# Inverse transforms fed by GpSimd: the second product over x's spectrum, raw weights behind GpSimd's additions, one output by SyncE, stores of v ahead of loads

## The chip, the cores and the metric

The kernel runs on one core of one Trainium2 chip. The metric is the device time of one execution in microseconds (us); lower is better. Matrix products run on TensorE (PE in the profile, PEld its weight loads), elementwise work on VectorE (DVE), ScalarE (ACT) and GpSimd (POOL), and SyncE (SP) issues most of the transfers. Each engine takes its own instructions strictly in the order in which the program has them.

## The reference

Two branches work on the same normalised input and are summed: a long convolution (S4D) done by FFT, and a gated feed-forward layer (GLU). There are 2048 positions, D = 448 channels, N = 256 states and F = 1792 hidden units, all in float32.

```python
xn = _layernorm(x, axis=-1)                     # x: [1, 2048, 448]
# S4D
P = jnp.exp((A * dt[:, None])[:, :, None] * pos[None, None, :])
K = 2.0 * jnp.einsum("dn,dnl->dl", C, P).real   # kernel of 2048 taps per channel
Kf, Uf = jnp.fft.rfft(K, 2 * L), jnp.fft.rfft(u_t, 2 * L)
y = jnp.fft.irfft(Uf * Kf[None, :, :], 2 * L)[:, :, :L]
# GLU
h = sigmoid(xn @ w_gate) * (xn @ w_up)
return x + (y + xn * D_skip) + h @ w_down
```

## The kernel before, in words

The program has two generators, `conv` and `glu`, whose instructions are interleaved by a planner: each `yield` names a cost, and the generator that is further behind its total goes on. A scheduler then orders the instructions of each engine by priority and by the pairs that `tc.issue_after` fixes.

The GLU runs over two halves of the positions (each two blocks `t` of 512) and over F in chunks `f` of 128 hidden units. For each pair (f, t) `gate` makes two sums of 11 matmuls of 128x512 (gate and up, tile `gu`, L710). Float32 is split into a high part and a remainder, so each weight chunk has two tiles, `wh` and `wl`, and of the 11 matmuls the first four read `wh`, the next four `wl`. The down projection reads `dh` and `dl` in the same way (tile `po`, L831). In the first half the split weights of some chunks are stored and read back later. The chunks in `RAW` (0, 1, 2, 4, 5) are not: in the second half their raw weights are loaded again by GpSimd's queue (`wraw`, `rdw`), and GpSimd makes `wh` by a copy and `wl` by a subtraction (L774, L775), and `dh`, `dl` alike (L802, L803). They are the last five chunks of the second half, in the order 4, 5, 0, 1, 2, and the code below makes each of them just ahead of the gate that reads it first.

The convolution first makes the taps (until about 530 us), and then `spectra` does the transforms beside the GLU's last chunks. It has 17 steps (h, k), numbered 0 to 16 here: h is the half of the channels, k a group of four frequency blocks; step 1 is the odd one (None, 32), with 64 rows. A step has these parts:

- `there` (L902): 64 small matmuls turn the loaded rows `skl` and `sx` into the spectra of taps and x in the two PSUM tiles `pk` and `px`; ScalarE copies the odd parts (`oo`), and VectorE makes `kk` and `xx` (L924, L925).
- `product` (L929): two VectorE products over 896 columns (L931, L932), then a subtraction and an addition of 448 columns on GpSimd (L934, L935) give the complex product `yy`. The second product is written over `kk`, of which there is one buffer.
- `halves` (L938): VectorE makes `sd` from `yy` (L940, L941), one step later.
- `back` (L944): 32 matmuls on `sd` go back to the time side, again into `pk` and `px`; ScalarE copies them to `vt`, and SyncE stores `vt` to `v_d` in DRAM (L973).
- `turned` (L975): SyncE reads rows of two steps back as `vp`, and `last` (L981) does the final matmuls (L989) and adds the result to `acc`, which `out` and `out_end` store.

On TensorE the order of a step is `there` of step n, one or two gate sums or down products, `back` of step n-2, more of the GLU, and so on; this order is fixed by the `issue_after` marks `sp_mm` and `glu_mm`.

Of the kernel before, what the change touches and what calls it, by code (L numbers as in the profile page):

```python
# [15 lines left out]
ALU = mybir.AluOpType  # L16
# [24 lines left out]
H = D // 2  # L41
# [86 lines left out]
def s4d_glu_kernel(ctx, tc, io):  # L128
    nc = tc.nc
    hp = tc.high_priority  # L130
    v = nc.vector
# [565 lines left out]
    def gate(w, xs, to, between=None):  # L697
# [30 lines left out]
            v.tensor_tensor(hl, hf, hh, ALU.subtract)  # L728
        to.append((hh, hl))

    def glu():
        stores, later, coming, coming_d = [], [], {}, {}
        last_fs = [f for fs_ in ORDER[1] for f in fs_]
        follow = dict(zip(last_fs, last_fs[1:]))
        for half in range(2):
# [4 lines left out]
            for fs_ in ORDER[half]:  # L740
# [14 lines left out]
                for n_, (f, t) in enumerate(order):  # L755
                    if t == 0:
                        wh = pg.tile([128, 2, 4, 128], F32R, name="wh", bufs=2)
                        if half == 0:
                            first = len(raws) == 2
                            raw, rd = raws.pop()  # L760
                            wl = w_low()
                            with hp(HP):
                                nc.scalar.copy(wh, raw)
                                if first:
                                    v.scalar_tensor_tensor(wl, raw, lim[:, 0, 0:1], wh, ALU.mult, ALU.subtract)
                                else:
                                    v.tensor_tensor(wl, raw, wh, ALU.subtract)
                            if not raws and f + 1 < NFT:
                                raws.append((w_load(f + 1), None))
                            if f not in RAW:  # L770
                                stores.extend(kept((wh, wl), wt_d, f))
                        elif f in RAW:
                            raw, wl = coming.pop(f), w_low()
                            nc.gpsimd.tensor_copy(wh, raw)  # L774
                            nc.gpsimd.tensor_tensor(wl, raw, wh, ALU.subtract)  # L775
                        else:
                            wl = w_low()
                            for t_, d_ in kept((wh, wl), wt_d, f):
                                nc.sync.dma_start(t_, d_)
                        if half == 1 and follow.get(f) in RAW:  # L780
                            coming[follow[f]] = w_load(follow[f], eng=nc.gpsimd)
                        ws.append((wh, wl))
                    between = (lambda s_=mid[n_]: step(*s_)) if cross and mid[n_] else None
                    yield from gate(ws[f - f0], xq[2 * half + t], hs[t], between)
                    for t_, d_ in stores:
                        nc.sync.dma_start(d_, t_)
                    stores[:] = later
                    later.clear()
                    if t == 0:
                        dh = pg.tile([128, D], F32R, name="dh", bufs=FCH[0])  # L790
                        if half == 0:
                            rd = rd or rd_load(f)
                            dl = d_low()
                            with hp(HP), tc.issue_after((act if f == 1 else marks)[0].ins):
                                nc.scalar.copy(dh, rd)
                            nc.gpsimd.tensor_tensor(dl, rd, dh, ALU.subtract)  # L796
                            if f not in RAW:
                                later.extend(kept((dh, dl), dt_d, f))
                        elif f in RAW:
                            dl = d_low()  # L800
                            rd = coming_d.pop(f)
                            nc.gpsimd.tensor_copy(dh, rd)  # L802
                            nc.gpsimd.tensor_tensor(dl, rd, dh, ALU.subtract)  # L803
                        else:
                            dl = d_low()
                            for t_, d_ in kept((dh, dl), dt_d, f):
                                nc.sync.dma_start(t_, d_)
                        if half == 1 and follow.get(f) in RAW:
                            rd = pg.tile([128, D], F32, name="rdw", bufs=1)
                            coming_d[follow[f]] = rd_load(follow[f], rd, nc.gpsimd)  # L810
                        wts.append((dh, dl))
                    yield 2.5
                    for s_ in end[n_] if cross else ():
                        step(*s_)
                    if cross:
                        yield 2
# [38 lines left out]
    def spectra(pf):  # L855
# [16 lines left out]
        def work(n, sh, bufs):  # L872
            return spare[n].pop() if spare.get(n) else pf.tile(sh, F32, name=n, bufs=bufs)
# [28 lines left out]
        def there(k, tb, sk, sx):  # L902

            n = 2 if k == 32 else 4
            np_ = 32 * n
            both = []
            for j, src in enumerate((sk, sx)):
                with after():
                    for c in range(2):
                        for g in range(n):  # L910
                            for p in range(2):
                                s = slice(64 * p, 64 * p + 64)
                                to = pb[j][32 * g : 32 * g + 32, p, H * c : H * c + H]
# [4 lines left out]
                                mm = nc.tensor.matmul(to, w, rhs, start=True, stop=True, skip_group_check=True)  # L918
                sp_mm[:] = [mm]
                ev, od = (half(pb[j][:np_, p, : 2 * H]) for p in range(2))  # L920
                oo = work("oo", [128, 2, H], 2)
                nc.scalar.copy(oo[:np_], od)
                t = work(("kk", "xx")[j], [128, 2, 2, H], 1)
                v.tensor_tensor(t[:np_, 0], ev, oo[:np_], ALU.add)  # L924
                read = v.tensor_tensor(t[:np_, 1], ev, oo[:np_], ALU.subtract)  # L925
                both.append(t[:np_])
            return *both, read

        def product(np_, kk, xx, eng=nc.gpsimd):  # L929
            yy = work("yy", [128, 2, 2, H], 1)[:np_]  # L930
            v.tensor_tensor(yy, kk, xx, ALU.mult)  # L931
            v.tensor_tensor(kk, kk, xx[:, :, ::-1], ALU.mult)  # L932
            with hp(HP):
                eng.tensor_tensor(yy[:, :, 0], yy[:, :, 0], yy[:, :, 1], ALU.subtract)  # L934
                eng.tensor_tensor(yy[:, :, 1], kk[:, :, 0], kk[:, :, 1], ALU.add)  # L935
            return yy

        def halves(np_, yy):  # L938
            sd = work("sd", [128, 2, 2, H], 2)
            v.tensor_tensor(sd[:np_, 0], yy[:, 0], yy[:, 1], ALU.add)  # L940
            v.tensor_tensor(sd[:np_, 1], yy[:, 0], yy[:, 1], ALU.subtract)  # L941
            return sd

        def back(h, k, sd, engs=(nc.sync, nc.sync)):  # L944
# [30 lines left out]
        def turned(h, k, n=8):  # L975
            if h not in vp:
                vp[h] = pf.tile([128, 32, H], F32, name="vp", bufs=1)
            s = slice(k // 4, 128, n)
            nc.sync.dma_start(vp[h][s], v_d[h, s])

        def last(h, q):  # L981
# [16 lines left out]
                v.tensor_tensor(a, a, half(pb[q % 2][:, p, : 2 * H]), ALU.add)  # L998
            if h == 1 and q < 3:
                out_end(acc, 4 * q, ds, *([[nc.gpsimd]] if q == 0 else []))  # L1000
            elif h == 0 and q < 2:
                out(acc, 4 * q, h)

        ac = acl[0]
        lasts.append(last)
# [9 lines left out]
        for n, (h, k) in enumerate(steps):  # L1015
# [8 lines left out]
            prev = h, k, 64 if k == 32 else 128  # L1024
            prev += (product(prev[2], kk, xx, v if end else nc.gpsimd),)
            if (h, k) == (0, ks[-NTB - 1]):
                for k_ in ks[:-NTB]:
                    tabs.pop(k_)
# [23 lines left out]
            if due and n >= due[0]:  # L1052
                sp_mm[:] = glu_mm
                for q in (0, 1, 2, 3)[2 * (n - due[0]) : 2 * (n - due[0]) + 2]:
                    sp_mm[:] = glu_mm
                    last(0, q)
                    yield WS / 2
                if n == due[0] + 1:
                    due = []
        sp_mm[:] = glu_mm  # L1060
        back(*made)
        sp_mm[:] = glu_mm
        back(*made_, (nc.sync, nc.scalar))
        for t in (*wait, made[:2], made_[:2]):
            turned(*t)

    def conv():
        with tc.tile_pool(name="psk", bufs=1, space=PSUM) as ps_, tc.tile_pool(
# [89 lines left out]
    lasts, glu_mm, sp_mm, glu_on, outs, x1s, hfs, xls = [], [], [], [], [0], [0], [], []  # L1158
# [45 lines left out]
```

## Time and profile before

| what | value |
|---|---|
| median of 3 runs | 746.65 us (744.72 to 747.68) |
| the profiled execution | 741.93 us, of it 740.1 us from the first to the last instruction |
| granted TensorE clock, mean | 0.949 |
| busy: PE, DVE, ACT, POOL | 90%, 79%, 57%, 57% of the span |
| DMA | 114.47 MB, mean 155 GB/s |
| `spectra` on TensorE | about 541 to 703 us, then the last down products and `last` |

All times inside the run are us from the start of the span. A row of the timeline has start, length, engine, line, operation, output and input tiles with their shape, and in brackets how long the engine stood idle ahead of it and what ended that. A row of the waits reads: engine and line that waited, arrow, whom it waited for, then total us, times, and the longest. A row of the stretches (windows) gives the busy time of each engine, the granted TensorE clock (PEclk), the busy share of the DMA engines and GB/s. "Issue" as a releaser means that the profile shows none.

### The profile page before, as it was taken

To read this page: it belongs to the slowest core of one execution; us is meant where nothing else is said; L and a number is where in the kernel's file an instruction comes from. 1 tells how busy PE (TensorE), PEld (TensorE's weight loads), DVE (VectorE), ACT (ScalarE), POOL (GpSimd) and SP (SyncE) were. 2 spreads that over 40 slices of the span, in tenths; PEclk is the share of its full clock that TensorE was granted. 3 is DMA by queue.
4 is the path that set the end of the run, shared out by engine and by line. 5 is a ranking of instruction groups with operands and counts; after the bars stand their busy time and mean duration, and the time that the engine had idled before them with its cause. 6 is when DMAs were issued, how large, how long until landed. Compare 5 with 4: busy or idle time off the path is not lost.

```text
span 740.1 us, 20863 instructions
## 1 busy us (share of the span) xinstructions
PE 668.2 (90%) x8581; PEld 515.1 (70%) x8581; DVE 587.9 (79%) x779; ACT 420.6 (57%) x651; POOL 420.8 (57%) x453
## 2 busy tenths in 40 slices
PE   2998999988999999788999999999988999788976
PEld 1765878866877787555878888888765667466655
DVE  5799998699999999886679898886757777756833
ACT  3655454689778789887387777777323322222310
POOL 2120116869999999974645776765537773541301
PEclk9999999995999999999999999999998989898987
DMA  9935338451313564354863323322669887874464
GB/s 199 235 114 198 116 102 263 147 188 58 126 48 97 175 191 116 114 181 148 264 188 99 93 95 95 99 81 83 157 171 266 222 244 185 262 210 130 125 169 132
DMA packets 94335, 114.47 MB, mean 155 GB/s; under 512 B 13728, under 2 KB 83936, under 8 KB 93984
## 3 DMA queue, kind: packets, MB, share of 16 engines
q1 hardware_dynamic: 72512, 92.54, 43.1%
q10 hardware_dynamic: 19248, 14.91, 7.0%
q0 software_dynamic: 2480, 5.67, 3.0%
q8 instruction: 68, 1.11, 0.6%
q14 instruction: 27, 0.22, 0.1%
HBM read 68.32 MB, written 44.76 MB: 153 GB/s over the span
## 4 chain that ended last, share of the span: by engine, by line
PE 40%; POOL 19%; issue 11%; DVE 11%; DMA 11%; SPq 5%; ACT 3%; POOLq 0%; DVEq 0%; ACTq 0%
PE gu L710 17%; PE po L831 10%; POOL me L513 7%; PE ko L619 5%; POOL mf L513 5%; PE tr L535 2%; DMA v_d<-vt 2%; POOL dl L796 2%; DVE Ft L605 2%; DVE Et L604 1%; DMA skl<-sk_d 1%; SPq L896 1%; DMA xe<-in_A_u_dram 1%; DVE Et L603 1%; POOL yy L934 1%
## 5 line engine op out<-in xcount | busy, mean ns | idle before, releaser
L513 POOL TENSOR_TENSOR me<-me,pm 128x32 f32<-128x32 f32 (+1 forms) x168 | 149.5, 890 | 67.6 <-DVE Et L604 57.8
L513 POOL TENSOR_TENSOR mf<-mf,pm 128x64 f32<-128x64 f32 (+1 forms) x112 | 118.8, 1061 | 5.3
L710 PE MATMUL gu<-xh,wh 128*128 128x512 f32 x336 | 103.2, 415 | 3.0 <-ACT th L718 1.2
L710 PE MATMUL gu<-xl,wh 128*128 128x512 f32 x336 | 97.7, 394 | 0.0
L710 PE MATMUL gu<-xh,wl 128*128 128x512 f32 x336 | 96.5, 395 | 0.0
L604 DVE TENSOR_TENSOR Et<-me,S 128x1024 f32<-128x1024 f32 x56 | 80.4, 1436 | 13.9 <-ACT me L526 9.0
L831 PE MATMUL po<-dh,hh 128*128 128x448 f32 (+1 forms) x227 | 87.4, 385 | 0.8 <-DVE acc L836 0.8
L605 DVE TENSOR_TENSOR Ft<-mf,S 128x1024 f32<-128x1024 f32 x56 | 83.8, 1496 | 5.1 <-PE ko L619 3.2
L831 PE MATMUL po<-dh,hl 128*128 128x448 f32 (+1 forms) x227 | 84.5, 374 | 2.0 <-DVE hl L728 2.0
L831 PE MATMUL po<-dl,hh 128*128 128x448 f32 (+1 forms) x227 | 84.8, 374 | 0.2 <-POOL dl L796 0.2
L603 DVE TENSOR_TENSOR Et<-me,S 128x1024 f32<-128x1024 f32 x56 | 77.5, 1385 | 4.0 <-ACT S L546 3.5
L710 PEld LDWEIGHTS gu<-xh,wh 128*128 128x128 f32 x336 | 62.6, 195 | 25.8 <-issue 6.9
L543 ACT ACTIVATE S<-tr 128x1024 f32<-128x1024 f32 x56 | 57.9, 1033 | 34.4 <-PE tr L535 18.7
L619 PEld LDWEIGHTS ko<-Et,Ft 128*32 128x32 f32 x3584 | 56.0, 114 | 28.0 <-issue 10.5
L619 PE MATMUL ko<-Et,Ft 128*32 128x64 f32 x3584 | 66.0, 227 | 9.7 <-DVE Ft L605 5.3
L710 PEld LDWEIGHTS gu<-xh,wl 128*128 128x128 f32 x336 | 63.8, 191 | 14.9 <-DVE hl L728 0.7
L710 PEld LDWEIGHTS gu<-xl,wh 128*128 128x128 f32 x336 | 63.0, 189 | 14.8 <-issue 1.4
L726 ACT CAST hh<-gu 128x512 fp32r<-128x512 f32 x56 | 33.1, 591 | 69.8 <-DVE gu L721 68.8
L836 DVE SCALAR_TENSOR_TENSOR acc<-po,acc 128x448 f32<-128x448 f32 (+1 forms) x81 | 48.7, 613 | 28.2 <-PE po L831 27.9
L934 POOL TENSOR_TENSOR yy<-yy 128x448 f32<-128x448 f32 (+1 forms) x16 | 28.5, 1778 | 67.1 <-DVE yy L931 66.9
L546 ACT ACTIVATE S<-S,hpi 128x1024 f32<-128x1024 f32 x56 | 65.6, 1171 | 0.0
L718 ACT ACTIVATE th<-gu 128x512 f32<-128x512 f32 x56 | 33.9, 606 | 43.5 <-PE gu L710 43.5
(214 smaller groups left out, 1346.7 us busy)
## 6 DMA issues: line engine op xcount, KB each, us to landing
sk_d<-sk ACTq DMA_DIRECT2D x14, 512.0 KB
sx<-x_d SPq DMA_DIRECT2D x64, 112.0 KB
skl<-sk_d SPq DMA_DIRECT2D x64, 112.0 KB
v_d<-vt SPq DMA_DIRECT2D x27, 224.0 KB
vp<-v_d SPq DMA_DIRECT2D x6, 896.0 KB
wt_d<-wh SPq DMA_DIRECT2D x9, 512.0 KB
wt_d<-wl SPq DMA_DIRECT2D x9, 512.0 KB
wl<-wt_d SPq DMA_DIRECT2D x9, 512.0 KB
```

The costliest lines, as they stand in the source:

```text
L513: ins = nc.gpsimd.tensor_tensor(m[:, :, w + a : 2 * w : n], m[:, :, a:w:n], par(base + i).unsqueeze(2).to_broadcast([128, 4 * DC, w // n]) ...
L543: nc.scalar.activation(rows(cs), pv, AF.Abs)
L546: sins[:] = [nc.scalar.activation(cs, cs, AF.Sin, scale=-TWO_PI, bias=hpi)]
L603: v.tensor_tensor(Et[:, :, :, 32:64], two(me[:, :, 32:64]), S[:, 1::-1], ALU.mult)
L604: v.tensor_tensor(Et[:, :, :, 0:32], two(me[:, :, 0:32]), S[:, 1:3, :, ::-1], ALU.mult)
L605: fts[:] = [v.tensor_tensor(Ft, two(mf), S[:, 3:5], ALU.mult)]
L619: nc.tensor.matmul(ko[32 * j : 32 * j + 32, sl], Ft[:, cc, DC * h + 4 * q + j], Et[:, cc, DC * h + 4 * q + j], start=(k == 0), stop=(k == ...
L710: glu_mm[:] = [nc.tensor.matmul(ps, a_, b_, start=(n == 0), stop=(n == len(mm) - 1))]
L718: marks[0] = nc.scalar.activation(th, pgu[0], AF.Tanh, scale=0.5)
L831: glu_mm[:] = [nc.tensor.matmul(po[:, ds], a_[:, bs], w_[:, ds], start=(n == 0), stop=(n == 3 * fc - 1))]
L836: v.scalar_tensor_tensor(acc[:, b, ds], po[:, ds], 0.5, acc[:, b, ds], ALU.mult, ALU.add)
L934: eng.tensor_tensor(yy[:, :, 0], yy[:, :, 0], yy[:, :, 1], ALU.subtract)
```

## The change

It has five parts.

1. The second product is written over `xx` and not over `kk`; `xx` gets three buffers instead of one, and `halves` writes its sums over `xx` too, so that `sd` and its two buffers go. `kk` keeps its one buffer.
2. GpSimd's splitting of the raw weights (`wh`, `wl`, `dh`, `dl` of the chunks in `RAW`, second half) is placed behind `made_by`, GpSimd's last addition that the code has emitted when it comes to the chunk.
3. The output of the first two blocks of the first channel half goes out by SyncE alone, two calls of `last` later; before, SyncE, ScalarE and GpSimd took turns.
4. At the end the load of `vp` for steps 13 and 14 is one transfer placed ahead of the last two `back`s; the stores of the last two follow each other, and one load fetches the rows of both.
5. The rest are names that follow.

```diff
+    def behind():
+        return tc.issue_after(made_by[0].ins) if made_by else nullcontext()
...
                         elif f in RAW:
                             raw, wl = coming.pop(f), w_low()
-                            nc.gpsimd.tensor_copy(wh, raw)
-                            nc.gpsimd.tensor_tensor(wl, raw, wh, ALU.subtract)
+                            with behind():
+                                nc.gpsimd.tensor_copy(wh, raw)
+                                nc.gpsimd.tensor_tensor(wl, raw, wh, ALU.subtract)
...
-                            nc.gpsimd.tensor_copy(dh, rd)
-                            nc.gpsimd.tensor_tensor(dl, rd, dh, ALU.subtract)
+                            with behind():
+                                nc.gpsimd.tensor_copy(dh, rd)
+                                nc.gpsimd.tensor_tensor(dl, rd, dh, ALU.subtract)
...
-                t = work(("kk", "xx")[j], [128, 2, 2, H], 1)
+                t = work(("kk", "xx")[j], [128, 2, 2, H], (1, 3)[j])
...
-            v.tensor_tensor(kk, kk, xx[:, :, ::-1], ALU.mult)
+            v.tensor_tensor(xx, kk[:, :, ::-1], xx, ALU.mult)
             with hp(HP):
                 eng.tensor_tensor(yy[:, :, 0], yy[:, :, 0], yy[:, :, 1], ALU.subtract)
-                eng.tensor_tensor(yy[:, :, 1], kk[:, :, 0], kk[:, :, 1], ALU.add)
-            return yy
-
-        def halves(np_, yy):
-            sd = work("sd", [128, 2, 2, H], 2)
-            v.tensor_tensor(sd[:np_, 0], yy[:, 0], yy[:, 1], ALU.add)
-            v.tensor_tensor(sd[:np_, 1], yy[:, 0], yy[:, 1], ALU.subtract)
+                made_by[:] = [eng.tensor_tensor(yy[:, :, 1], xx[:, :, 0], xx[:, :, 1], ALU.add)]
+            return yy, xx
+
+        def halves(yy, sd):
+            v.tensor_tensor(sd[:, 0], yy[:, 0], yy[:, 1], ALU.add)
+            v.tensor_tensor(sd[:, 1], yy[:, 0], yy[:, 1], ALU.subtract)
             return sd
...
-            elif h == 0 and q < 2:
-                out(acc, 4 * q, h)
+            elif h == 0 and q > 1:
+                out_end(ac[:, 4 * q - 8 : 4 * q - 4], 4 * q - 8, ds, [nc.sync])
...
+        turned(*wait[0], 4)
         sp_mm[:] = glu_mm
         back(*made)
         sp_mm[:] = glu_mm
         back(*made_, (nc.sync, nc.scalar))
-        for t in (*wait, made[:2], made_[:2]):
-            turned(*t)
+        turned(*made[:2], 4)
```

VectorE, ScalarE and TensorE keep their orders, apart from the three output stores that leave ScalarE and from some matmuls inside a few `back`s that change places with each other. What moves is the order of GpSimd and a few rows of SyncE.

GpSimd before, from the subtraction of step 1: the split of chunk 5 (`wh_7184`, `wl_7185`) stands between and behind the two additions of step 1, and its successor's loads follow at once.

```order
L934 TENSOR_TENSOR yy_6849<-yy_6849 64x2x224
L774 CAST wh_7184<-wraw_6889 128x1024
L935 TENSOR_TENSOR yy_6849<-kk_6830 64x2x224
L775 TENSOR_TENSOR wl_7185<-wraw_6889,wh_7184 128x1024
L645 DMA wraw_7188<-in_B_w_gate_dram 128x3x128
L647 DMA wraw_7188<-in_B_w_gate_dram 64x128 x2
L645 DMA wraw_7188<-in_B_w_up_dram 128x3x128
L647 DMA wraw_7188<-in_B_w_up_dram 64x128 x2
L934 TENSOR_TENSOR yy_6953<-yy_6953 128x2x224
L935 TENSOR_TENSOR yy_6953<-kk_6926 128x2x224
L934 TENSOR_TENSOR yy_7060<-yy_7060 128x2x224
L935 TENSOR_TENSOR yy_7060<-kk_7033 128x2x224
```

GpSimd in the change, the split of the same chunk 5 (now `wh_7180`, `wl_7181`), with the additions of steps 3 (`yy_7057`) and 4 (`yy_7163`) ahead of it:

```order
L939 TENSOR_TENSOR yy_7057<-yy_7057 128x2x224
L940 TENSOR_TENSOR yy_7057<-xx_7052 128x2x224
L939 TENSOR_TENSOR yy_7163<-yy_7163 128x2x224
L940 TENSOR_TENSOR yy_7163<-xx_7158 128x2x224
L778 CAST wh_7180<-wraw_6888 128x1024
L807 CAST dh_7244<-rdw_6991 128x448
L779 TENSOR_TENSOR wl_7181<-wraw_6888,wh_7180 128x1024
L808 TENSOR_TENSOR dl_7245<-rdw_6991,dh_7244 128x448
```

The split has moved three steps later, from step 1 to behind the additions of step 4. In the same way chunk 4 now comes behind step 1, chunk 0 behind step 10, chunk 1 behind step 12 and chunk 2 behind step 14.

TensorE at the same place in the change (before, the rows are the same with other buffer numbers): `there` of step 4, the gate that reads chunk 5 first, and `back` of step 2.

```order
L923 MATMUL pk_6704<-skl_6854,tb_6859 32x224 x16
L923 MATMUL px_6705<-sx_6853,tb_6859 32x224 x16
L710 MATMUL gu_7191<-xh_3575,wh_7180 128x512 x3
L710 MATMUL gu_7191<-xr_3577,wh_7180 128x512
L710 MATMUL gu_7191<-xh_3575,wl_7181 128x512 x3
L710 MATMUL gu_7191<-xr_3577,wl_7181 128x512
L710 MATMUL gu_7191<-xl_3576,wh_7180 128x512 x3
L957 MATMUL pk_6704<-xx_6946,bk_6702 64x224 x4
L957 MATMUL px_6705<-xx_6946,bk_6702 64x224 x4
```

Nothing has moved here: the gate that reads `wh_7180` stands directly behind `there` of step 4, whose `px` is an input of `yy_7163`. The first gates of chunks 0 and 2 stand directly behind `there` of steps 10 and 14 in the same way; that of chunk 4 has one gate sum between, that of chunk 1 two gate sums, one `back` and one `last`.

SyncE at the end, before (stores of steps 13 to 16 and their loads; 16 rows a load for the last four):

```order
L973 DMA v_d_64<-vt_8539 32x8x224 x2
L979 DMA vp_8452<-v_d_64 16x7168
L973 DMA v_d_64<-vt_8630 32x8x224 x2
L979 DMA vp_8452<-v_d_64 16x7168
L973 DMA v_d_64<-vt_8665 32x8x224 x2
L979 DMA vp_8452<-v_d_64 16x7168
L973 DMA v_d_64<-vt_8686 32x8x224
L979 DMA vp_8452<-v_d_64 16x7168
```

And in the change:

```order
L977 DMA v_d_64<-vt_8524 32x8x224 x2
L977 DMA v_d_64<-vt_8614 32x8x224 x2
L983 DMA vp_8438<-v_d_64 32x7168
L977 DMA v_d_64<-vt_8649 32x8x224 x2
L977 DMA v_d_64<-vt_8670 32x8x224
L983 DMA vp_8438<-v_d_64 32x7168
```

Two loads have gone from between the stores, and each of the two that are left has 32 rows.

More of the change, by code (lines that the diff above doesn't have):

```diff
@@ L1023, in spectra @@
                     made = *prev[:2], halves(*prev[2:])
-            prev = h, k, 64 if k == 32 else 128
-            prev += (product(prev[2], kk, xx, v if end else nc.gpsimd),)
+            prev = h, k, *product(64 if k == 32 else 128, kk, xx, v if end else nc.gpsimd)
             if (h, k) == (0, ks[-NTB - 1]):
@@ L1156, in conv @@
             yield from spectra(pf)
-    lasts, glu_mm, sp_mm, glu_on, outs, x1s, hfs, xls = [], [], [], [], [0], [0], [], []
+    made_by, lasts, glu_mm, sp_mm, glu_on, outs, x1s, hfs, xls = [], [], [], [], [], [0], [0], [], []
     xq, psc, raws, acl, marks, slots, pqs = list(x_first), [], [], [], [None, None], {}, []
```

## The prediction

> **What bounds the kernel now.** I read the waits first, then the timeline of TensorE, then the stretches for the granted clock. The change touches nothing that runs before about 541 us, so only `spectra` (541 to 703 us) and the end count.
>
> ```profile
> 541.00:703.00 162.00, 143.34 (x1956) 99.43 (x1954) 116.82 (x172) 43.88 (x84) 78.93 (x69) 0.91 0.73 202
> ```
>
> TensorE is busy for 143.3 of these 162 us, VectorE for 116.8, GpSimd for 78.9. So TensorE bounds the stage, and it stands idle for 18.7 us. The waits say where:
>
> ```profile
> DVE kk L924 <- POOL yy L935: 18.8, 10, 3.3
> PE pk L953 <- DVE kk L925: 10.8, 5, 5.1
> PE pk L989 <- issue: 6.8, 1, 6.8
> ...
> PE pk L918 <- DMA skl<-sk_d: 1.3, 2, 1.1
> ```
>
> VectorE cannot write the one `kk` until GpSimd's addition has read it, 18.8 us in ten waits; `back` cannot overwrite `pk` until `kk` has been made from it, so 10.8 us of waiting reach TensorE. The 6.8 us stand ahead of `last` at the end. Loads cost it 1.3 us. The single stops of `back`, with the one that has "issue":
>
> ```profile
> 560.25 0.99 PE L953 MATMUL pk<-sd,bk 32*64 32x224 f32 x16 [1.50 <-issue]
> 595.03 0.99 PE L953 MATMUL pk<-sd,bk 32*64 32x224 f32 x16 [1.30 <-DVE kk L925]
> 641.45 1.40 PE L953 MATMUL pk<-sd,bk 32*64 32x224 f32 x12 [5.09 <-DVE kk L925]
> 666.72 0.99 PE L953 MATMUL pk<-sd,bk 32*64 32x224 f32 x16 [2.43 <-DVE kk L925]
> ```
>
> A stop costs more than its length, since the granted clock (seventh number after the length, 1.00 is full) falls behind it:
>
> ```profile
> 560.00:575.00 15.00, 12.97 (x158) 9.07 (x166) 11.90 (x18) 3.65 (x7) 9.94 (x11) 0.77 1.00 293
> 595.00:604.00 9.00, 8.89 (x106) 5.79 (x107) 6.32 (x10) 1.99 (x4) 5.71 (x4) 0.62 0.93 241
> ...
> 642.00:648.00 6.00, 6.00 (x98) 3.35 (x91) 4.80 (x5) 1.99 (x4) 4.05 (x4) 0.54 0.68 216
> ...
> 664.00:675.00 11.00, 8.49 (x69) 5.44 (x75) 7.06 (x10) 3.45 (x7) 2.29 (x2) 0.69 0.72 183
> ...
> 724.00:730.00 6.00, 6.00 (x129) 3.75 (x117) 3.42 (x6) 0.00 (x0) 2.18 (x4) 0.54 0.22 51
> ```
>
> Length times missing clock gives what each slow stretch loses: 3.5, 3.4, 2.8, 3.4 and 2.8 us.
>
> **Part 1, the second product over `xx`.** No instruction is added or removed; `kk` no longer waits for GpSimd. The stops at 560, 595 and 666 go (1.5, 1.3, 2.4 us; the one at 666 also needs part 3). At 641 `back` follows `there` with no gate between, so some 1.5 us stay for the copy `oo` and two `kk`, and 3.6 go. Together 8.8 us, with 6 to 14 us as the ends (only the stops of the two largest, or nearly all idle time of the stage). With them go the slow stretches at 595 and 664, 6.8 us (0 to 10 us). That is the gain. GpSimd's wait moves to the halves, four VectorE instructions later, where it costs nothing as long as TensorE is the bound. `back` then reads sums two steps old.
>
> **Part 2, the raw weights behind the additions.** This is the part that decides. TensorE takes its instructions in order, and the gate that reads a new `wh` first stands directly behind `there` of step n for chunks 5, 0 and 2, while `wh` now stands behind GpSimd's addition of the same step n. So TensorE must wait through the whole product of step n before it gets a weight that was ready long ago before: `there`, `oo`, `kk`, `xx`, sums, product, two GpSimd operations, copy, subtraction. The length of this chain, from rows of step 0, which had no wait in it, of the sums (absent in step 0) and of the split:
>
> ```profile
> 542.75 0.96 PE L918 MATMUL px<-sx,tb 64*32 64x224 f32 x32
> 549.17 1.15 POOL L935 TENSOR_TENSOR yy<-kk 128x448 f32<-128x448 f32 x1
> 570.43 0.61 DVE L940 TENSOR_TENSOR sd<-yy 128x448 f32<-128x448 f32 x1
> 571.62 1.09 DVE L931 TENSOR_TENSOR yy<-kk,xx 128x896 f32<-128x896 f32 x1
> 576.03 1.04 POOL L774 CAST wh<-wraw 128x1024 fp32r<-128x1024 f32 x1
> 577.15 2.40 POOL L775 TENSOR_TENSOR wl<-wraw,wh 128x1024 fp32r<-128x1024 f32 x1
> 534.04 0.57 POOL L802 CAST dh<-rdw 128x448 fp32r<-128x448 f32 x1
> ```
>
> From the end of `there` (543.71) to the end of the addition (550.32) are 6.6 us; the sums add 571.62 - 570.43 = 1.2; the copy 1.04. So `wh` is there 8.85 us after `there` ends. `wl` follows 2.45 us later, or 3.05 with the copy of `dh` between. Where the gates stand now:
>
> ```profile
> 548.02 1.07 PE L918 MATMUL px<-sx,t 64*32 64x224 f32 x13
> 551.65 0.84 PE L710 MATMUL gu<-xh,wh 128*128 128x512 f32 x3
> ...
> 576.12 0.98 PE L710 MATMUL gu<-xh,wh 128*128 128x512 f32 x3
> ...
> 577.17 0.85 PE L710 MATMUL gu<-xh,wl 128*128 128x512 f32 x3
> ...
> 645.70 1.74 PE L918 MATMUL px<-sx,tb 64*32 64x224 f32 x32
> ...
> 657.07 0.96 PE L710 MATMUL gu<-xh,wh 128*128 128x512 f32 x3
> ```
>
> The four matmuls on `wh` take 1.05 us (576.12 to 577.17), then the gate waits for `wl`. Chunks 5, 0 and 2: 8.85 us, and 3.05 - 1.05 = 2.0 more, 10.85 each, 32.6 in all. Chunk 4 has a gate sum between (549.09 to 551.65, 2.56 us): 6.3 and 1.4, so 7.7. Chunk 1 has 647.44 to 657.07, 9.6 us: no wait for `wh`, 0.6 for `wl`. Together 41 us of new idle time. Its ends: 36 if the sums are done while `xx` is made and `dh` slips behind `wl`; 46 if the odd copies stand behind other work of ScalarE. Queued behind each waiting gate are the other gate sum, `back` of step n-2 and `there` of the next step, and with them VectorE and all transfers of later steps; nothing of the GLU passes a waiting gate, so no cover is left.
>
> The clock falls behind these stops. Behind the stop of 6.8 us at the end it cost 2.8 us; here a third of that falls into the wait for `wl`, so I take 2.0 for chunks 5, 0 and 2, 6 in all (2 to 10), and none for chunk 4, whose slow stretch stands in place of the one at 560.
>
> The Trainium skill, "TensorE: Matmul & The Clock Gate", section "Part 1: The HAM clock gate", says that the clock halves after an idle window of about 3.4 us and is full again after about 3.4 us of work. By that a short stop would cool nothing and a long one cost an estimated 1.7 us; the trace disagrees on the first, with 0.62 behind a stop of 1.30 us. By the page the sum would be 41 + 3 x 1.7 - 8.8 - 3.5, some 34 us.
>
> GpSimd's own work is the same. Its additions gain the time that splits took ahead of them; this hides behind TensorE. The next `wraw` is loaded later, but one step or more ahead of its use.
>
> **Part 3, the output by SyncE.**
>
> ```profile
> 659.49 4.71 ACTq L236 DMA_DIRECT2D out_dram<-ac  x3
> ...
> 661.82 2.69 SPq L236 DMA_DIRECT2D out_dram<-ac  x3
> 664.62 2.37 SPq L896 DMA_DIRECT2D skl<-sk_d  x4
> ...
> 697.28 0.99 PE L918 MATMUL pk<-skl,tb 64*32 64x224 f32 x32
> ```
>
> ScalarE loses 4.7 us of issuing, which is what held `oo` back ahead of the stop at 666 (counted). SyncE issues eight at 0.9 us, 7.2 for 2.7, so the loads of step 16 at 664 start 4.5 us later; `there` of step 16 is at 697, which hides them. Nothing more: 0.
>
> **Part 4, stores ahead of loads.** The end of the chain before:
>
> ```profile
> 708.42 0.59 SPq L973
> ...
> 709.05 4.50 DMA v_d<-vt
> ...
> 713.61 0.52 SPq L979
> ...
> 714.23 4.58 DMA v_d<-vt
> 718.81 4.96 issue
> 723.77 1.78 PE pk L989 x32
> ...
> 709.54 0.54 ACT L959 COPY vt<-px 128x448 f32<-128x448 f32 x1
> ```
>
> The last store (714.23) stood behind a load that waited for the store ahead of it. Now it is issued right behind that one, when its `vt` is there (709.54 + 0.54), and lands at about 715; one load of 32 rows (5.15 us by the row below, against 4.96) ends at about 720.3. Gain 3.5 us; 0 if the stores share bandwidth so that the last lands as late as now, 4.6 if nothing is shared.
>
> ```profile
> 626.41 5.15 DMA vp<-v_d
> ```
>
> **The sum**, against the profiled execution of 741.93 us: +41 + 6 - 8.8 - 6.8 - 3.5 = +27.9, 769.8 us. That execution lies 4.7 us under the median of the three runs (746.65), so the median to expect is about 774.
>
> **Rivals.** (a) *Faster.* TensorE comes to the gates when the split is done, because the chain is mostly over by then. Then only gains are left, -8.8 - 6.8 - 3.5 = -19.1, and the median is 727.5. It decides where the four stops average under 4.8 us (19.1 / 4). For it speaks only that TensorE is the busiest engine; against it the two orders, in which `there` and the gate are neighbours, so TensorE cannot be late. (b) *The stops replace nearly all idle time and slow stretches of the stage* and transfers that run on during them make the rest quicker: gains of 14 + 10 + 4.6 against 36 + 2, +9, median 756. For it speaks a DMA share of 0.73; against it the 1.3 us that TensorE waits for loads. (c) *The short stops are not what slows the clock*: no slow stretch goes, +34, median 781. For it the stretch at 560 with DMA at 1.00, against it the full clock wherever there was no stop. (d) *The chain is longer than in step 0*, since ScalarE's `hh` and GpSimd's loads stand in it: 46 + 10 - 6 - 3.5, +46, median 793. (e) The change does nothing visible: splits are hidden and `kk` was not the limit, 746.
>
> **How the numbers follow.** The forecast has 0.52, (b) 0.17, (c) 0.15, (d) 0.10, (a) 0.04, (e) 0.02. From 754 to 790 I leave out (a), (e), a third of (b) and most of (d), together some 0.19. Slower by over 0.5% (3.7 us, about what a measurement of this kernel tells from no change): all but (a) and (e), 0.94.
>
> **What would show it.** Right: `gu` waiting for GpSimd's `wh` and `wl` with some 40 us in all, four stops of 6 to 9 us, each behind a `there`; `kk` waiting for GpSimd no more and the halves in its place; at the end two stores in a row and some 3 us less ahead of `last`. Wrong: gates that start right behind `there`, or `back` still waiting 10 us for `kk`. The forecast fails if TensorE's stops are under 5 us each.

## The result, and the profile after

The changed kernel takes 767.4 us (median of 4 runs, 765.48 to 767.93) against 747.16 us of the kernel before on the same chip: a ratio of 1.0267, 95% interval 1.0230 to 1.0304. It is slower by 20 us. The profiled execution took 767.62 us (span 765.8), 25.7 us more than that of before.

The waits of TensorE from 544 to 745 us in the kernel after (total us, times, longest). The first two rows did not exist before; `kk`, which cost 10.8 us, costs 3.4:

```profile
PE gu L710 <- POOL wh L778: 32.9, 5, 9.1
PE gu L710 <- POOL wl L779: 3.8, 5, 1.2
PE pk L957 <- DVE kk L930: 3.4, 2, 1.7
PE pk L923 <- ACT vt L963: 3.1, 3, 1.4
```

One such stop in the timeline of the kernel after, chunk 5: the rows of TensorE and then those of GpSimd (start, length, what ran, in brackets the idle time ahead and what ended it):

```profile
582.30 0.96 PE L923 MATMUL px<-sx,tb 64*32 64x224 f32 x32
592.41 1.65 PE L710 MATMUL gu<-xh,wh 128*128 128x512 f32 x3 [9.14 <-POOL wh L778]
...
595.23 1.65 PE L710 MATMUL gu<-xh,wl 128*128 128x512 f32 x3 [0.75 <-POOL wl L779]
```

```profile
590.25 1.13 POOL L940 TENSOR_TENSOR yy<-xx 128x448 f32<-128x448 f32 x1
591.32 1.04 POOL L778 CAST wh<-wraw 128x1024 fp32r<-128x1024 f32 x1
...
592.82 2.36 POOL L779 TENSOR_TENSOR wl<-wraw,wh 128x1024 fp32r<-128x1024 f32 x1
```

`there` ends at 583.26. Until 592.41 TensorE does nothing: it waits for the addition at 590.25 and the copy behind it. The raw weights had been in place for some 20 us: GpSimd issued their loads by 567.65, and such a load lands 4.3 to 4.5 us after its issue (median). Five places look like this, with stops ahead of `wh` of 5.86, 9.14, 8.73, 0.80 and 8.39 us (chunks 4, 5, 0, 1, 2).

The stage as a row of the stretches (length; busy time of TensorE, its loads, VectorE, ScalarE, GpSimd, each with instructions; clock, DMA share, GB/s), from the first matmul of step 1 to the end of the last `back` but one, the same 1928 matmuls: the kernel before, then the kernel after, here with the stretch from there to the first matmul of `last`:

```profile
544.88:707.43 162.55, 144.93 (x1928) 100.87 (x1928) 119.14 (x175) 42.75 (x83) 78.37 (x68) 0.91 0.73 202
```

```profile
548.52:735.03 186.51, 140.26 (x1928) 97.77 (x1928) 117.69 (x175) 42.89 (x83) 89.24 (x80) 0.86 0.64 179
...
735.03:749.78 14.75, 9.05 (x69) 7.58 (x69) 2.95 (x5) 1.94 (x4) 0.57 (x1) 0.91 0.72 218
```

The stage is 24.0 us longer: TensorE's idle time goes from 17.6 to 46.3 us (+28.6), its busy time falls by 4.7. The wait for the last rows goes from 16.3 us (707.43 to 723.77) to 14.75. The first row starts 3.6 us later; ahead of it both kernels run the same instructions, so this belongs to the execution and not to the change.

### The profile page after: what moved, and what is told of

It is laid out like the page before. It is cut to its first block, busy times and chain, and to the rows that moved or that the text cites. A ratio compares the mean times of both kernels' runs of the same rounds, so it can differ in the third digit from the quotient of the medians.

```text
span 765.8 us, 20857 instructions
## 1 busy us (share of the span) xinstructions
PE 667.4 (87%) x8581; PEld 513.4 (67%) x8581; DVE 581.0 (76%) x779; ACT 421.1 (55%) x651; POOL 418.1 (55%) x450
## 4 chain that ended last, share of the span: by engine, by line
PE 43%; POOL 17%; DVE 12%; issue 11%; DMA 8%; ACT 4%; SPq 4%; POOLq 0%; DVEq 0%; ACTq 0%
PE gu L710 17%; PE po L836 11%; POOL me L513 7%; PE ko L619 5%; POOL mf L513 4%; PE tr L535 2%; POOL dl L800 2%; POOL wl L779 2%; DVE Ft L605 1%; PE pk L957 1%; DVE gu L721 1%; DVE Et L604 1%; DMA xe<-in_A_u_dram 1%; PE pk L923 1%; DVE Et L603 1%
## 5 line engine op out<-in xcount | busy, mean ns | idle before, releaser
L710 PE MATMUL gu<-xh,wh 128*128 128x512 f32 x336 | 105.2, 421 | 37.8 <-POOL wh L778 32.9
L513 POOL TENSOR_TENSOR mf<-mf,pm 128x64 f32<-128x64 f32 (+1 forms) x112 | 115.9, 1035 | 5.3
L710 PE MATMUL gu<-xh,wl 128*128 128x512 f32 x336 | 99.9, 406 | 3.8 <-POOL wl L779 3.8
L710 PE MATMUL gu<-xl,wh 128*128 128x512 f32 x336 | 100.0, 402 | 0.0
L721 DVE SCALAR_TENSOR_TENSOR gu<-th,gu 128x512 f32<-128x512 f32 x56 | 38.5, 688 | 67.1 <-PE gu L710 60.3
L605 DVE TENSOR_TENSOR Ft<-mf,S 128x1024 f32<-128x1024 f32 x56 | 80.7, 1440 | 7.2 <-PE ko L619 4.3
L543 ACT ACTIVATE S<-tr 128x1024 f32<-128x1024 f32 x56 | 57.9, 1034 | 33.9 <-PE tr L535 18.5
L710 PEld LDWEIGHTS gu<-xl,wh 128*128 128x128 f32 x336 | 65.0, 195 | 15.6 <-issue 1.4
```

The source lines that it names most:

```text
L513: ins = nc.gpsimd.tensor_tensor(m[:, :, w + a : 2 * w : n], m[:, :, a:w:n], par(base + i).unsqueeze(2).to_broadcast([128, 4 * DC, w // n]) ...
L543: nc.scalar.activation(rows(cs), pv, AF.Abs)
L605: fts[:] = [v.tensor_tensor(Ft, two(mf), S[:, 3:5], ALU.mult)]
L710: glu_mm[:] = [nc.tensor.matmul(ps, a_, b_, start=(n == 0), stop=(n == len(mm) - 1))]
L721: marks[1] = v.scalar_tensor_tensor(hf, th, 1.0, pgu[1], ALU.add, ALU.mult)
```

## The experiments

**Without the wait (part 2 taken out).** The kernel after with `behind` empty:

```diff
     def behind():
-        return tc.issue_after(made_by[0].ins) if made_by else nullcontext()
+        return nullcontext()
```

> The changed kernel without its part 2: the splits of the raw weights are free to stand where the scheduler puts them, as before. If the wait for weights behind the step's own addition is the whole loss, TensorE waits for no wh and no wl, kk waits for GpSimd no more, and the time falls below the kernel before by what parts 1 and 4 bring: some 9 us of stops of back, about 7 us of slow clock and 1.6 to 3.5 us at the end, so 726 to 733 us. If instead the new home of the second product or the three xx buffers themselves slow the stage, it stays at 745 us or above. If the short stops are not what slows the clock, the stretches at 595 and 664 stay slow and it is about 735.

731.18 us (728.55 to 734.28), ratio to before 0.9828 (0.9771 to 0.9885). The rest of the change is a gain of 14.5 us, and part 2 alone turns it into a loss: 36.2 us between the two. TensorE's waits in this kernel hold no `wh` or `wl` (one profiled execution):

```profile
PE pk L923 <- ACT vt L963: 8.1, 3, 5.0
...
PE pk L957 <- DVE kk L930: 3.4, 2, 1.7
```

**Behind the addition of the step before.** The wait stays, but on an addition one step older:

```diff
-                made_by[:] = [eng.tensor_tensor(yy[:, :, 1], xx[:, :, 0], xx[:, :, 1], ALU.add)]
+                made_by.append(eng.tensor_tensor(yy[:, :, 1], xx[:, :, 0], xx[:, :, 1], ALU.add))
...
-        return tc.issue_after(made_by[0].ins) if made_by else nullcontext()
+        return tc.issue_after(made_by[-2].ins) if len(made_by) > 1 else nullcontext()
```

> The changed kernel with the splits behind the additions of the step before, one step earlier than in the change. A step is 6 to 9 us of TensorE's time, the chain from there to wh took 8.4 to 9.1 us. If the loss is this chain against TensorE's order, the five waits for wh fall from 33 us to under 5 us in all, and wl adds 2 to 6 us: 730 to 742 us. If being behind additions at all is what costs (GpSimd's queue too full), most of the loss stays: over 755 us.

734.34 us (733.78 to 737.6), ratio 0.9865 (0.9820 to 0.9911). Its waits:

```profile
PE gu L710 <- POOL wh L778: 4.3, 2, 2.2
PE gu L710 <- POOL wl L779: 3.6, 2, 2.0
```

36.7 us of waiting at the gates become 7.9. It is not the ordering on GpSimd that costs, but that the addition belongs to the step whose `there` stands directly ahead of the gate.

**Only `dh` and `dl` behind the additions.** The kernel after, `wh` and `wl` free:

```diff
-                            with behind():
+                            with nullcontext():
                                 nc.gpsimd.tensor_copy(wh, raw)
                                 nc.gpsimd.tensor_tensor(wl, raw, wh, ALU.subtract)
```

> The kernel after, but only dh and dl stand behind GpSimd's additions; wh and wl are free. Theory (part 2 loses because a gate sum waits for wh and wl through the whole chain from there to the addition): dh and dl are read by the down product, which comes a gate sum and more later, so nothing waits for them: as the kernel after without part 2, 729 to 735 us. Rival (GpSimd's queue as such: whatever is pinned behind an addition delays the splits that follow it): wh and wl of the next chunk still come late, TensorE stops 15 us or more at gu, 745 to 757 us.

733.43 us (730.75 to 735.32), ratio 0.9851 (0.9809 to 0.9893): as without part 2. TensorE waits for no split. The loss lies in `wh` and `wl`.

**Part 2 alone, on the kernel before.** The same `behind` in the kernel before, nothing else.

> The kernel before with part 2 alone. With the theory: five waits for wh and wl as in the changed kernel, some 37 to 40 us (the chain is a little longer, since kk also waits for GpSimd there), less the idle time of back that the stops replace; with the stops of 595 and 666 and the end left as before, 775 to 790 us. If parts 1, 3 and 4 bring nothing, it equals the changed kernel, 767 us.

776.32 us (774.75 to 777.89), ratio 1.0420 (1.0375 to 1.0465), +30.6 us. Its waits, of TensorE and of VectorE:

```profile
PE gu L710 <- POOL wh L778: 32.4, 4, 9.9
PE gu L710 <- POOL wl L779: 3.9, 5, 1.3
```

```profile
DVE kk L929 <- POOL yy L940: 10.4, 7, 2.3
```

The stops are those of the kernel after, 36.3 us; that `kk` waits for GpSimd again, 10.4 us, does not lengthen them.

**Part 1 alone, on the kernel before** (the second product over `xx`, three buffers, sums in its place).

> The kernel before with part 1 alone: second product over xx, three xx buffers, sums in its place. If kk's wait for GpSimd is what stopped back: those waits go, 10.8 us of stops become 2 to 4 us, and the slow stretch at 595 goes; the one at 666 also hangs on ScalarE's three output stores and may stay. 731 to 739 us. If VectorE's wait only moves to the sums and TensorE is then held by them, no change: 745 to 748 us.

745.3 us (744.43 to 749.71), ratio 1.0012 (0.9985 to 1.0038): nothing, where 731 to 739 was expected. TensorE's waits in the stage, and ScalarE's for the stores of `vt`, in this kernel:

```profile
PE pk L952 <- DVE kk L925: 9.3, 3, 6.0
PE pk L918 <- ACT vt L958: 9.0, 4, 3.4
```

```profile
ACT vt L958 <- DMA v_d<-vt: 16.3, 3, 7.5
```

VectorE no longer waits for GpSimd, but TensorE still waits, a little later. `there` overwrites what the last `back` left, so it waits for the copies `vt`; the copies wait for a buffer, of which there are two, until its store has landed (before: TensorE 1.7 us for `vt`, and ScalarE 3.2 us ahead of `vt`, which the profile puts down to loads of `sx`). And the longest wait for `kk` is now at 669.76, since `oo` stands behind three output stores that ScalarE issues (SyncE's row stands first):

```profile
664.46 0.43 SPq L892 DMA_DIRECT2D tb<-in_c_tab_dram  x1
664.50 2.80 ACTq L236 DMA_DIRECT2D out_dram<-ac  x3
667.41 0.60 ACT L718 ACTIVATE th<-gu 128x512 f32<-128x512 f32 x1 [12.81 <-DMA tb<-in_c_tab_dram]
667.90 0.53 ACT L922 COPY oo<-pk 128x448 f32<-128x448 f32 x1
```

```profile
669.76 1.39 PE L952 MATMUL pk<-xx,bk 32*64 32x224 f32 x12 [5.97 <-DVE kk L925]
```

Issuing the stores takes 2.80 us of it. The sums that they store were done by 657.99, and yet they are issued only at 664.50, right behind SyncE's load of `tb`, which the profile names as what ended ScalarE's wait of 12.81 us although `th` does not read it. Why the stores waited for that is open, so part of the loss in this kernel is not explained.

**Part 3 alone, on the kernel before:**

```diff
-            elif h == 0 and q < 2:
-                out(acc, 4 * q, h)
+            elif h == 0 and q > 1:
+                out_end(ac[:, 4 * q - 8 : 4 * q - 4], 4 * q - 8, ds, [nc.sync])
```

> The kernel before with part 3 alone: the first output by SyncE. ScalarE no longer stands 4.7 us in its stores, so the stop of 2.4 us at 666 and its slow clock should get smaller. The prediction counted this under part 1, and nothing for part 3. If ScalarE's stores are a limit of their own: 740 to 744 us, the stop at 666 under 1 us, and kk then waits for GpSimd. If GpSimd's wait on kk holds that stop anyway: 745 to 747 us.

736.48 us (734.81 to 741.05), ratio 0.9877 (0.9840 to 0.9914): -8.7 us (-6.4 to -11.9 by the interval). The part that was given nothing of its own is the largest gain. The copy `oo` of the kernel before, behind ScalarE's stores of 4.71 us, and then TensorE and ScalarE in this kernel:

```profile
664.79 0.53 ACT L922 COPY oo<-pk 128x448 f32<-128x448 f32 x1
```

```profile
660.54 0.99 PE L918 MATMUL pk<-skl,tb 64*32 64x224 f32 x32
661.63 0.53 ACT L922 COPY oo<-pk 128x448 f32<-128x448 f32 x1 [0.33 <-PE pk L918]
```

`oo` now starts 0.1 us after `there` has written `pk` (661.53); before, it began 4.0 us after (664.79 against 660.77). The `back` behind this `there` does not stop any more.

**Parts 1 and 3:**

> Parts 1 and 3 together, without 2 and 4. Part 1 alone measured no gain (745.3): its stops moved to the copy vt and to the odd copy behind ScalarE's stores, 6.0 us at 670. If the two parts hide each other, the pair gains most of what the kernel without part 2 gained (14.5 us) less the end: 732 to 737 us, without the stop of 6 us. If they only add up with part 3 alone, the pair equals part 3 alone.

732.89 us (730.29 to 736.97), ratio 0.9827 (0.9782 to 0.9872). With ScalarE's stores gone, part 1 seems worth 3.6 us more (736.48 to 732.89); the runs of the two kernels overlap, so this is not clear of the noise.

**Part 4 alone** (the loads and stores at the end):

> The kernel before with part 4 alone: at the end two loads of 32 rows in place of four of 16, and the last stores next to each other. The prediction gave it 3.5 us (0 to 4.6); the changed kernel's trace gives 1.6 us, since the load of 32 rows now runs beside the last stores. So -1.6 to -3.5 us: 742 to 744 us; the last matmuls start 14 to 14.5 us after the last but one back, before 15.8. If nothing waits for those stores, 746 us.

742.74 us, ratio 0.9976 (0.9948 to 1.0005): not clear of no change, -1.8 us by the difference of the ratio from 1. Its own trace, from the end of the last `back` but one to the first matmul of `last`:

```profile
712.58:724.97 12.39, 9.04 (x69) 7.58 (x69) 2.50 (x4) 1.93 (x4) 1.10 (x2) 1.00 0.78 250
```

That is 3.9 us less than the 16.3 before, where the kernel after has 1.6 less and the kernel without part 2 (695.75 to 710.20) 1.9. The execution as a whole is no shorter, because its stage starts 4.5 us later.

**The last stores ahead of the load of steps 13 and 14.** The kernel without part 2, with that load behind the last stores; this asks why part 4 gave less than 3.5 us:

```diff
-        turned(*wait[0], 4)
         sp_mm[:] = glu_mm
         back(*made)
         sp_mm[:] = glu_mm
         back(*made_, (nc.sync, nc.scalar))
+        with tc.issue_after(stored[0].ins):
+            turned(*wait[0], 4)
         turned(*made[:2], 4)
```

> The kernel without part 2 (731.2 us), with the load of the rows of steps 13 and 14 placed behind the last stores instead of ahead of them. If the last stores are slowed by that load beside them, they land 1 to 2 us sooner and the time falls to 729 to 730.5 us. If bandwidth is what counts, the load now stands ahead of the last one and the end is as late or later: 731 to 733 us.

731.49 us (730.08 to 735.62), ratio 0.9807 (0.9769 to 0.9846): no difference. The last store takes 6.62 us there and 5.45 without the move, so the place of that load in the queue is not what holds it.

Three runs went after the wait for `vt`. **Loads of `vp` one step later**, first without part 2, then with part 1 alone:

```diff
-            while len(wait) > 2 and not (due and wait[0][0] == 1):
+            while len(wait) > 3 and not (due and wait[0][0] == 1):
```

> The kernel after without part 2, and each load of vp in the loop one step later (the last of the first half moves one step with them). Theory (with kk free, back and there wait for the copies vt, and these for a buffer whose store waits in SyncE's queue behind loads of vp that wait for older stores to land): SyncE's wait of 17.6 us for stores falls under 6, ScalarE's 12.6 us for v_d<-vt under 5, TensorE's 8.1 us at L923 for vt under 4; 723 to 729 us. Rival (the stores take their time by bandwidth, whatever stands in the queue): ScalarE's wait stays at 10 us or more, 729 to 735 us.

> The kernel before with part 1, and each load of vp in the loop one step later. Part 1 alone gave nothing, 745.3 us. Theory (its gain is eaten by the stores of vt): ScalarE's 16.3 us of waiting for v_d<-vt fall under 6, TensorE's 9.0 us for vt under 4.5, 735 to 741 us. Rival (it is eaten by kk waiting for oo behind ScalarE's own output stores): TensorE's 9.3 us for kk stay, and the time with them, 742 to 747 us.

735.05 us (733.41 to 741.42), ratio 0.9891 (0.9834 to 0.9948), and 743.34 us, ratio 1.0009 (0.9970 to 1.0048). The theory fell in both: neither ScalarE's wait for the stores nor TensorE's for `vt` shrank. The rows of the first, then of the second:

```profile
ACT vt L963 <- DMA v_d<-vt: 18.4, 3, 7.8
```

```profile
PE pk L923 <- ACT vt L963: 10.8, 6, 3.7
```

```profile
ACT vt L958 <- DMA v_d<-vt: 23.1, 5, 8.3
```

```profile
PE pk L918 <- ACT vt L958: 11.2, 5, 5.8
PE pk L952 <- DVE kk L925: 5.0, 3, 1.7
```

In the second the rival fell too: the wait for `kk` went from 9.3 to 5.0 us, and the time did not follow. The execution in its trace, 737.55 us, is the fastest of its ten.

**A quarter of x's bytes.** Without part 2, as many loads of `sx`, but one block of four:

```diff
-                nc.sync.dma_start(sx[s], x1_d[r + k : r + k + 4, :, ds].rearrange("k b d -> b k d"))
+                nc.sync.dma_start(sx[s, :1], x1_d[r + k : r + k + 1, :, ds].rearrange("k b d -> b k d"))
...
-                                rhs = sx[s, g]
+                                rhs = sx[s, g if k == 32 else 0]
```

> The kernel after without part 2, with as many loads of sx but a quarter of their bytes: each step loads one of its four frequency blocks of x and uses it for all four, so x's spectrum is not the reference's. Theory (the stores of vt land late because the DMA engines are full, 0.78 of the stage's time without part 2, so the copies vt wait, and with them back and there): ScalarE's 12.6 us of waiting for v_d<-vt fall under 5, TensorE's 8.1 us for vt under 4, and most of its 4.5 us for skl go too; 720 to 727 us. Rival (a store takes as long whatever else is loaded, by its own packets or the order of the queue): ScalarE's wait stays at 10 us or more and TensorE's at 7 or more, only the wait for skl shrinks; 727 to 733 us.

726.56 us (725.46 to 734.52), ratio 0.9803 (0.9722 to 0.9884), and neither theory in full (the last row is the stretch of 544.71 to 695.75):

```profile
PE pk L923 <- ACT vt L963: 7.3, 5, 3.3
```

```profile
ACT vt L963 <- DMA v_d<-vt: 6.5, 1, 6.5
```

```profile
544.71:695.75 151.04, 135.31 (x1965) 97.59 (x1966) 120.18 (x177) 45.09 (x87) 76.12 (x66) 0.94 0.66 183
```

With the DMA engines 0.66 busy in the stage in place of 0.78, ScalarE's wait is 6.5 us in place of 12.6, one long wait is left, and TensorE's hardly moves (8.1 to 7.3). But in the kernel with the last stores moved, whose edit touches only the end, ScalarE's wait is 8.0 us at full traffic, so the step to 6.5 is not clear of what two executions differ by; nor is the time, since the intervals of 0.9803 and 0.9828 overlap. That traffic is part of why a store lands late is therefore not shown, and why the waits for `vt` arise stays open. A third buffer for `vt` would be the direct test; it was not tried.

The stage of the kernels in one view each, in this order: part 1, part 3, parts 1 and 3, without part 2, part 2 alone:

```profile
545.42:707.30 161.88, 137.60 (x1928) 98.26 (x1928) 118.82 (x172) 42.27 (x82) 79.62 (x68) 0.92 0.72 201
```

```profile
545.40:701.40 156.00, 141.44 (x1928) 99.07 (x1928) 119.25 (x174) 42.94 (x82) 77.72 (x66) 0.91 0.76 210
```

```profile
546.56:700.15 153.59, 135.09 (x1928) 96.00 (x1928) 118.88 (x172) 42.49 (x82) 78.39 (x66) 0.93 0.76 212
```

```profile
544.71:695.75 151.04, 133.41 (x1928) 96.21 (x1928) 118.70 (x175) 42.50 (x83) 75.39 (x66) 0.93 0.78 214
```

```profile
541.51:739.60 198.09, 149.65 (x1928) 102.20 (x1928) 117.00 (x175) 42.89 (x82) 90.33 (x82) 0.83 0.62 171
```

One profiled execution each, so that a few us between two rows are not clear of the noise. From these, and from the stage cut into stretches of 2 us, in each of which busy time is multiplied by the missing clock:

| kernel | length | TensorE idle | lost to the slow clock while busy |
|---|---|---|---|
| before | 162.6 | 17.6 | 14.2 |
| part 1 | 161.9 | 24.3 | 10.9 |
| part 3 | 156.0 | 14.6 | 11.2 |
| parts 1 and 3 | 153.6 | 18.5 | 8.2 |
| without part 2 (1, 3, 4) | 151.0 | 17.6 | 7.2 |
| part 2 alone | 198.1 | 48.4 | 22.0 |
| after | 186.5 | 46.3 | 13.3 |

## Why the prediction came out right, and which terms were off

774 us were predicted, within 754 to 790, slower with a chance of 0.94; 767.4 were measured. The mechanism was the one named: chain from `there` to the addition, then the copy, then the gate.

- **The stops at the gates: 41 us predicted, 36.7 measured** (6.2, 9.9, 9.5, 2.0 and 9.1 for chunks 4, 5, 0, 1 and 2). The wait for `wh` was right: 8.85 against 9.14, 8.73 and 8.39. The second wait was put at 2.0 and came out at 0.75, because the four matmuls ahead of it run at half clock (592.41 to 594.48, 2.07 us in place of 1.05). When `wl` is there is fixed by GpSimd; what the stop lost, the slow clock took.
- **The slow clock behind them: +6 predicted.** Between the kernel without part 2 and the kernel after it is 13.3 - 7.2 = 6.1 us. That the two agree is partly luck. The stretches behind chunks 5, 0 and 2 lost 3.6, 3.2 and 2.6 us and not 2.0 each, that behind chunk 4 lost 2.2 and not nothing, and 5.6 us of slow stretches that the kernel without part 2 has between 547 and 644 went in turn.
- **The slow stretches that go: -6.8 predicted.** Before to the kernel without part 2: 7.2 - 14.2 = -7.0, right in sum, and the two stretches that were named, at 595 and 664, are the ones that are gone. But 3.3 come with part 1 alone and 3.0 with part 3 alone: part 3 by itself takes the one at 664 (its clock is full from 650 to 696), and part 1 alone takes the one at 595 and has a new one of 3.0 at 622 to 630.
- **The stops of `back`, -8.8: the step that failed was to let them vanish.** In the kernel after TensorE's other idle time falls from 17.6 to 46.3 - 36.7 = 9.6 us, so 8.0 us did go. But 5.5 of them go with part 2 alone too (48.4 - 36.3 = 12.1), where `kk` still waits for GpSimd: there the new stops stand in the place of the old ones. Without part 2 the idle time is 17.6 as before, and with part 1 alone it is 6.7 us longer: the waits for `vt` and, with part 1 alone, for `oo` behind ScalarE's stores come in their place. So without part 2 the term of 8.8 gave nothing, the end 1.9 in place of 3.5, and 4.5 us of busy time that was not in the sum went instead; the gain was 14.5 us where the terms gave 19.1.
- **Part 3, 0 predicted, -8.7 measured alone.** Its stop of 2.4 us and the stretch of 3.4 behind it, 5.8 us, had been booked under part 1 with "also needs part 3". They need part 3 and do not need part 1. The other 3 us of the 8.7 are not accounted for; the two profiled executions differ by 5.4 us only.
- **Part 4, -3.5 predicted:** 1.6 in the trace of the kernel after, 1.9 without part 2, 3.9 in the trace of part 4 alone, whose time moved by 1.8. It lies between the two ends that were named, 0 and 4.6. In the kernel after the last store takes longer than the 4.50 and 4.58 before, and the load behind it 6.1 us (743.67 to 749.78) in place of 5.15; with part 4 alone the two take 4.3 and 5.3 (715.42, 719.69, 724.97). Why they differ was not found. The store of the kernel after:

```profile
737.71 5.91 DMA v_d<-vt
```

- **Not in the sum:** the 4.7 us of busy time that the stage lost are 0.9 of clock; 3.8 are left. In the kernel before a `back` behind its stop ran `pk` and `px` one after the other (560.25 to 562.33, 2.08 us); in the kernel after, one without a stop runs them in turns:

```profile
607.40 0.42 PE L957 MATMUL pk<-xx,bk 32*64 32x224 f32 x4
607.53 0.42 PE L957 MATMUL px<-xx,bk 32*64 32x224 f32 x4
...
608.12 0.40 PE L957 MATMUL px<-xx,bk 32*64 32x224 f32 x4
```

That is 1.12 us (607.40 to 608.52); 0.96 less at each of four such stops would make the 3.8. That fits, but no run tested it. By the rows of the stages the loss comes with part 1 alone (busy time -7.3, of it -3.3 clock) and with part 2 alone (+4.7, of it +7.8), and hardly with part 3 alone (-3.5, of it -3.0).

In sum: idle +28.6, clock -0.9, other busy time -3.8, the end -1.6 to -1.9, the start of this execution +3.6, together the 25.7 us by which the two spans differ.

The rivals: (a) fell, the four stops average 8.7 us, not under 4.8. (b) was half right on the stage's other idle time, which fell by 8.0 of 17.6 us. Its price, 756, was too low: its 36 us for the stops were right (36.7), but the slow clock behind them cost 6.1 and not 2, and the gains were some 20 us (8.0 idle, 7.0 clock, 3.8 busy time, 1.6 at the end) and not 28.6. (c) fell: the stretches at 595 and 664 went. (d) fell, no wait for `wh` exceeded 9.14 us. (e) fell.

## What to carry to other kernels

Where one engine's work is pinned behind a step, count the whole chain of that step from the point where the waiting engine feeds it: if the consumer stands right behind the chain's start in its queue, the wait is the chain's length, and pinning it to the step before costs little (here 3.2 us in place of 36.2). A buffer conflict that is removed can show the next one (here, by the profile, the two `vt` buffers and the stores behind them), so its stop is a gain only when the next release is known to be earlier. Transfers issued by an engine that also computes delay the computation behind them, and moving them to another queue can be worth more than the change beside it (here 8.7 us against nothing for part 1 alone).

## What was not expected of the hardware

The length of a stop alone does not set the clock. Two stretches of the kernel without part 2, the first with a stop and the second the work behind it:

```profile
596.40:598.02 1.62, 0.23 (x3) 0.00 (x1) 0.97 (x2) 1.07 (x3) 1.62 (x2) 1.00 0.95 265
598.02:605.00 6.98, 6.98 (x114) 5.54 (x114) 5.92 (x11) 2.42 (x5) 6.68 (x8) 1.00 0.77 205
```

The same place in the kernel before, the `back` behind the stop of 1.30 us (593.73 to 595.03) and the work that follows:

```profile
595.03:597.60 2.57, 2.49 (x32) 1.39 (x32) 2.54 (x5) 0.00 (x0) 0.00 (x0) 0.76 1.06 252
597.60:604.00 6.40, 6.40 (x77) 4.37 (x75) 3.75 (x6) 1.99 (x4) 5.71 (x4) 0.56 0.88 236
```

A stop of 1.39 us left the clock full; one of 1.30 us, with a `back` behind it whose two halves ran one after the other, was followed by a clock of 0.76 and then 0.56. The prediction's reading, that the stop of 1.30 us by itself slowed the clock, was too simple. Nor does such a `back` decide. In the kernel after two stops of 1.68 us, which end at 664.86 and at 728.32, have such a `back` behind them too, and these are the stretches that follow, with clocks of 1.00 and 0.70:

```profile
664.86:673.00 8.14, 8.06 (x141) 5.58 (x142) 7.93 (x13) 3.39 (x7) 3.21 (x2) 1.00 0.91 260
728.32:734.00 5.68, 5.60 (x49) 4.01 (x57) 5.54 (x9) 1.06 (x2) 0.00 (x0) 0.70 0.27 55
```

The stops of chunks 4, 5, 0 and 2 in the kernel after show when the clock falls, and for chunk 5 (583.26 to 592.41) when it comes back:

```profile
559.00:560.00 1.00, 0.00 (x0) 0.00 (x0) 0.63 (x1) 0.34 (x1) 0.92 (x2) 0.66 0.81 230
586.00:587.00 1.00, 0.00 (x0) 0.00 (x0) 0.96 (x3) 0.00 (x0) 0.00 (x0) 0.82 0.65 165
...
600.00:601.00 1.00, 1.00 (x11) 0.67 (x4) 0.00 (x0) 0.65 (x2) 0.41 (x1) 0.86 0.51 172
...
644.00:645.00 1.00, 0.00 (x0) 0.00 (x0) 1.00 (x3) 0.00 (x0) 0.00 (x0) 0.83 1.59 459
...
699.00:700.00 1.00, 0.00 (x0) 0.00 (x0) 0.74 (x2) 0.23 (x1) 0.00 (x0) 0.64 0.20 74
```

If the clock is either full or half, 0.82 means a fall at 586.64, 3.4 us after TensorE went idle, and 0.86 a return at 600.28, 5.1 us after the second gap of the gate ended (595.23) and 7.9 after its first matmul (592.41). The Trainium skill, "TensorE: Matmul & The Clock Gate", section "Part 1: The HAM clock gate", gives about 3.4 us for either. This stop agrees with the first and took longer for the second.

That the first agrees is chance, by the other stops: worked out in the same way, the clock falls at 559.32, 644.66 and 699.28, which is 3.8, 2.2 and 0.7 us after TensorE went idle (555.48, 642.49, 698.58; the last has a stop of 1.38 us just ahead). What the four falls share is their distance from each other: 27.32, 58.02 and 54.62 us, or 8, 17 and 16 times 3.41 us, and the return at 600.28 is 4 times 3.41 behind its fall. In the kernel before the falls at 562.22, 596.34, 640.72, 668.02 and 702.16 lie 10, 13, 8 and 10 times 3.41 us apart (from clocks of 0.61, 0.67, 0.86, 0.51 and 0.58 in the microsecond that holds each). So in these two traces the clock changes only at points of a grid of about 3.41 us, wherever a stop begins. A short stop can then be followed by a slow clock or not by where it falls on that grid, which would fit the pairs above; no run moved a stop along the grid to test it.
